# A planned attention-and-MLP block: another static order, zero products also ahead of side work, a norm chain without its copy, and a last tile whose norm and last product come in pieces

## The chip, the cores and the metric

The kernel runs on one core of one Trainium2 chip. The metric is the time of the whole execution on the device in microseconds, as the median of its runs. The engines are called as in the profile: PE is TensorE (matrix products, with PEld for its weight loads), ACT is ScalarE (activation functions), DVE is VectorE, POOL is GpSimd, and SP is SyncE, whose queue (SPq) issues nearly all transfers.

## The reference

One layer of a transformer with a grouped key and value (one for 32 heads) and a gated MLP; everything is bfloat16, with 2048 tokens of width 640.

```python
def _A_ref(x, wq, wk, wv, wo):          # H = 32 heads of Dh = 20, one k and one v for all
    q = (x @ wq).reshape(B, S, H, Dh).transpose(0, 2, 1, 3)
    k = x @ wk
    v = x @ wv
    scores = einsum("bhqd,bkd->bhqk", q, k) * (Dh ** -0.5)
    p = softmax(scores, axis=-1)
    o = einsum("bhqk,bkd->bhqd", p, v)
    return o.transpose(0, 2, 1, 3).reshape(B, S, H * Dh) @ wo
def _B_ref(x, w_gate, w_up, w_down):    # Dm = 640, Df = 1536
    return einsum("bsf,fd->bsd", gelu(x @ w_gate) * (x @ w_up), w_down)
x = A_x
h = x + _A_ref(layernorm(x), ...)
out = h + _B_ref(layernorm(h), ...)
```

## The kernel before

**Tiles and passes.** The tokens are cut into 16 tiles of 128 (`t`). A tile has two passes (`h` = 0, 1) of 16 heads, so there are 32 passes. In a pass the scores of the tile's queries against 16 blocks of 128 keys (`kt`) are formed in units: a unit is four heads against one block of keys, a matrix product on 32 rows of PE that fills one PSUM bank of 512 columns (line 940). Four units, one in each group of 32 rows, make a quad.

**Two ways of taking the exponential.** Most quads go to ACT: an activation Exp over two or three banks at once (line 1046, into `pbuf`). The string `D_QUADS` gives for each pass how many of the 16 quads go to DVE instead. There one TENSOR_SCALAR per unit (line 996) writes the bits of a power of two as integers (`dbuf`), and two shifted copies of the whole quad are made (`D_SHIFT`; line 1007 on DVE, or line 1011 on POOL for as many copies of a pass as `SHARE` allows), so that a weighted sum of three powers approximates the exponential. The products with the values (line 1160) then take one product per ACT quad and three per DVE quad; each is four matmuls on 32 columns of PE that run beside each other, added up in one PSUM bank.

**The rest of a tile** is called side work: the projection to q (two tiles ahead), the output projection and residual (lines 1265 to 1271), the second layer norm, the gate, up and down products (line 583 records all of these, since a helper `strips` issues them), the GELU by a tanh on ACT (line 1325) with its polynomial and its products on POOL or DVE (lines 1283 and 1285; `Z_POOL` and `H_POOL` choose by tile). Three operands per tile are transposed by a DMA from SP's queue: `onT<-oN` ahead of the output projection, `xnT<-xn_tmp` after the norm, `hhT<-g_us` ahead of the down product.

**The order.** Nothing is dynamic. A planner in the kernel's file (`_Sched.schedule`) takes every task with an estimated duration, simulates the five engines, and writes one fixed order for each. Its choices are steered by strings with one digit per pass: `PATIENCE`, `MARGIN`, `MARGIN_2` and `URGENT` (how long PE waits for score products, and what goes first), `D_AHEAD` and `D_BEFORE_END` (where a pass's DVE units are put among the cycles of score products), and by `LAG`, one digit per tile (0.05 us each, added to what the side work of that tile waits for in the plan). On the chip each engine runs its order, and a task waits on semaphores for what it needs. A PE task that is put too early therefore holds up everything behind it.

**Zero products.** Where the planner sees PE little used, it puts in a product of zeros (`filler`, four matmuls, planned at 0.215 us) that adds nothing to the open sum of the value products. The measure is `active`: PE's work in the last `WINDOW` = 3.42 us, where a score product counts as a quarter of its length. If it is below `least = 1.2 + 0.05 * FILL[phase]`, a zero product goes in, but only ahead of a score product (`t.cfg == "row"`).

**Norm.** The layer norm of a tile (`layer_norm`) is a chain over DVE and POOL: two BN_STATS and an aggregate on DVE, then on POOL a copy of the variance (`vb`, line 686, into `lnvb`), the addition of epsilon (`ve`, line 688), a power of one half (`pw`, line 690), and on DVE the reciprocal (`rc`) and the normalisation (`nm`, line 703).

**The last tile** (`last_tile`) has its own code: the output projection goes into the PSUM of the scores, the norm's chain is on DVE with the power on POOL (lines 1390 to 1402), PE transposes the result in two groups of 3 and 2 blocks (line 1420) that ACT and DVE evict (line 1427), and gate, up and down products run in three groups of four blocks of Df (lines 1445, 1472, 1477, 1454), the down product adding up in two halves of 320 columns, each of which is copied out and stored (lines 1488, 1490). Meanwhile PE works off what is left of tile 14's down product.

Of the kernel before, what the change touches and what calls it, by code (L numbers as in the profile page):

```python
# [6 lines left out]
ALU = mybir.AluOpType  # L7
# [4 lines left out]
P = 128  # L12
# [61 lines left out]
class _Sched:  # L74
# [8 lines left out]
    PATIENCE = "05456305540054532442603243443444"  # L83
    WINDOW, GAP = 3.42, 0.25
# [6 lines left out]
    FILL = "97755754644575535585755365355555"  # L91
# [45 lines left out]
    def schedule(self):  # L137
# [126 lines left out]
        while left:  # L264
# [202 lines left out]
def bass_sequential_preLN__grouped_kv_mqa__glu_gated_geglu__prompt_kernel(  # L467
# [74 lines left out]
    lnvb = sb("lnvb", [P, 4])  # L542
# [68 lines left out]
    LAG = "3434134353324532"  # L611
# [62 lines left out]
    def layer_norm(tag, t, src_deps, xnT_free, by_pe=None, fused=False):  # L674
# [11 lines left out]
        vb = add("pool", lambda e: e.tensor_copy(lnvb[:, ln.index:ln.index + 1], mv[:, ln.index, 1:2]), 0.2, [ag],  # L686
                 name=f"{tag}vb_{t}")
        ve = add("pool", lambda e: e.tensor_scalar(lnve[:, ln.index:ln.index + 1], lnvb[:, ln.index:ln.index + 1],
                                                   EPS, None, ALU.add), 0.2, [vb], name=f"{tag}ve_{t}")
        pw = add("pool", lambda e: e.tensor_tensor(lnden[:, ln.index:ln.index + 1],  # L690
                                                   lnve[:, ln.index:ln.index + 1], halfc[:], ALU.pow),
                 0.58, [ve, t_half], name=f"{tag}pw_{t}")
# [477 lines left out]
    URGENT = "45535357546755554446532554357655"  # L1170
# [106 lines left out]
    H_POOL = "1111111010011000"  # L1277
    Z_POOL = "0111010010011010"
# [72 lines left out]
    def last_tile(t, ont):  # L1351
# [45 lines left out]
        vb = add("dve", lambda e: e.tensor_copy(one(lnvb), mv[:, ln.index, 1:2]), 0.15, [ag], name=f"bvb_{t}")  # L1397
        ve = add("dve", lambda e: e.tensor_scalar(one(lnve), one(lnvb), EPS, None, ALU.add), 0.15, [vb], name=f"bve_{t}")
# [3 lines left out]
        nm = add("dve", lambda e: e.tensor_scalar(xn_tmp[:, xs.index, :], xh[:, t, :], mean(), one(lnr), ALU.subtract,  # L1402
# [37 lines left out]
        def job(wsb, i, bk):  # L1440
            def fn(e):
# [5 lines left out]
                return ins  # L1447
            return fn

        def down(i, j, c0, c1):  # L1450
            def fn(e):
                ins = None
                for fc in range(4 * i, 4 * i + 4):
# [272 lines left out]
```

## Time and profile before

| | us |
|---|---|
| median of 3 runs | 758.59 |
| lowest and highest run | 758.22 and 759.76 |
| the profiled execution's own time | 757.13 |
| span of its trace | 755.8 |
| PE busy | 719.4 (95%) |
| ACT busy | 724.4 (96%) |
| DVE busy | 667.9 (88%) |
| POOL busy | 271.7 (36%) |

The busy times come from one profiled execution; the span is from its first to its last instruction, and the execution's own time is 1.33 us longer. A busy PE is not PE at its peak, since the ends of matmuls are modelled, and four matmuls on 32 columns each can run beside each other. In the views, a time in brackets with an arrow is idle time of the engine just before the instruction, and names what ended it.

### The profile page before, as it was taken

What the parts mean: (1) busy time and instruction counts of PE and PEld (TensorE: products, weight loads), DVE (VectorE), ACT (ScalarE), POOL (GpSimd) and SP (SyncE); (2) the same over time, 40 slices, a digit from 0 to 9 for tenths busy, and PEclk for the clock granted to TensorE, in tenths of its full rate; (3) what the DMA queues carried; (4) which work ended last, traced back from release to release, by engine and by line L of the source; (5) the groups of instructions that cost most, each with busy time, mean ns of one, the idle gap of its engine ahead of it and who ended that gap; (6) DMA issues with size and microseconds to landing.
All of it is one profiled execution on the core that took longest, in us unless ns stands there. A gap on an engine that the chain in (4) does not pass through costs nothing.

```text
span 755.8 us, 24045 instructions
## 1 busy us (share of the span) xinstructions
PE 719.4 (95%) x10730; PEld 260.0 (34%) x10730; DVE 667.9 (88%) x1245; ACT 724.4 (96%) x698; POOL 271.7 (36%) x291
## 2 busy tenths in 40 slices
PE   9898999999998999999999999999999989999987
PEld 4422233333332333333333323333342323323336
DVE  8789999999998889999998899999989899888963
ACT  6999999999999999999999999999999999999982
POOL 5431315225355254324563234423232532450220
PEclk9999999999999999999999999999999999999999
DMA  7667002010113012111201102201130111010110
GB/s 181 128 218 192 10 10 45 11 30 6 31 33 45 19 23 43 27 30 10 45 3 40 33 11 46 41 20 24 23 55 20 16 20 23 19 31 19 35 33 20
DMA packets 79952, 31.53 MB, mean 42 GB/s; under 512 B 70880, under 2 KB 78560, under 8 KB 79840
## 3 DMA queue, kind: packets, MB, share of 16 engines
q1 hardware_dynamic: 78528, 29.86, 18.6%
q8 instruction: 85, 1.39, 0.7%
q10 hardware_dynamic: 1312, 0.05, 0.1%
q14 instruction: 27, 0.22, 0.1%
HBM read 10.21 MB, written 2.62 MB: 17 GB/s over the span
## 4 chain that ended last, share of the span: by engine, by line
ACT 44%; PE 41%; DVE 9%; DMA 3%; POOL 1%; issue 1%; SPq 0%; DVEq 0%
ACT pbuf L1046 42%; PE ps L583 15%; PE ps L940 14%; PE ps L1160 11%; DVE dbuf L996 3%; DVE dbuf L1007 2%; DMA onT<-oN 2%; ACT g_z L1325 1%; PE ps L1445 1%; DMA xh<-in_A_x_dram 1%; DMA xnT<-xn_tmp 1%; DVE stats L680 1%; DVE xn_tmp L703 1%; DVE stats L682 1%; POOL g_us L1285 0%
## 5 line engine op out<-in xcount | busy, mean ns | idle before, releaser
L1046 ACT ACTIVATE pbuf<-ps 128x1024 bf16<-128x1024 f32 (+1 forms) x656 | 696.6, 1218 | 9.6 <-PE ps L940 8.2
L996 DVE TENSOR_SCALAR dbuf<-ps 128x512 int16<-128x512 f32 x532 | 350.2, 680 | 40.5 <-PE ps L940 36.7
L940 PE MATMUL ps<-qT,kT 32*128 32x512 bf16 x2048 | 281.7, 387 | 16.9 <-ACT pbuf L1046 11.2
L940 PEld LDWEIGHTS ps<-qT,kT 32*128 32x128 bf16 x2048 | 73.6, 91 | 255.6 <-ACT pbuf L1046 189.7
L1007 DVE TENSOR_SCALAR dbuf<-dbuf 128x2048 int16<-128x2048 int16 x216 | 147.6, 700 | 0.8
L1160 PE MATMUL ps<-pbuf,v_ext 128*32 128x512 bf16 (+3 forms) x2052 | 144.5, 331 | 2.7 <-ACT pbuf L1046 1.7
L1160 PE MATMUL ps<-dbuf,v_w 128*32 128x512 bf16 x1596 | 139.6, 383 | 4.6 <-DVE dbuf L1007 3.3
L1011 POOL TENSOR_TENSOR dbuf<-dbuf,shifts 128x1024 int32<-128x1024 int32 x50 | 97.3, 1954 | 100.6 <-DVE dbuf L996 100.6
L1313 POOL TENSOR_TENSOR g_z<-g_gs 128x512 bf16<-128x512 bf16 x45 | 49.5, 1101 | 122.4 <-DVE g_gs L1311 122.1
L583 PE MATMUL ps<-wg_sb,xnT 128*32 128x512 bf16 x900 | 71.1, 389 | 0.5 <-DVE dbuf L996 0.2
L1160 PEld LDWEIGHTS ps<-pbuf,v_ext 128*32 128x32 bf16 x2052 | 44.9, 95 | 70.7 <-issue 49.2
L583 PE MATMUL ps<-wd_sb,hhT 128*32 128x320 bf16 x1440 | 67.6, 301 | 0.1
L583 PE MATMUL ps<-wu_sb,xnT 128*32 128x512 bf16 x900 | 66.8, 382 | 0.5 <-DVE dbuf L996 0.4
L1160 PEld LDWEIGHTS ps<-dbuf,v_w 128*32 128x32 bf16 x1596 | 39.5, 95 | 42.8 <-DVE dbuf L1007 15.7
L1285 POOL TENSOR_TENSOR g_us<-g_z,g_us 128x512 bf16<-128x512 bf16 x30 | 34.6, 1178 | 38.3 <-DVE g_z L1328 33.3
L1186 POOL TENSOR_TENSOR oN<-oT,rL 128x320 bf16<-128x320 f32 x30 | 21.8, 728 | 63.1 <-DVE rL L1181 63.0
L686 POOL CAST lnvb<-mv 128x1 bf16<-128x1 f32 x31 | 9.7, 313 | 96.0 <-DVE mv L684 95.9
L583 PEld LDWEIGHTS ps<-wd_sb,hhT 128*32 128x32 bf16 x1440 | 31.9, 96 | 25.3 <-issue 15.3
L1319 DVE SCALAR_TENSOR_TENSOR g_us<-ps,g_gs 128x512 bf16<-128x512 f32 x45 | 30.6, 679 | 6.0 <-PE ps L583 5.9
L1285 POOL TENSOR_TENSOR g_z<-g_z,g_gs 128x512 bf16<-128x512 bf16 x24 | 27.5, 1172 | 19.7 <-DVE g_z L1322 19.7
L583 PE MATMUL ps<-wo_sb,onT 128*32 128x320 bf16 x600 | 30.3, 304 | 4.5 <-DMA onT<-oN 3.8
L1311 DVE CAST g_gs<-ps 128x512 bf16<-128x512 f32 x45 | 30.5, 678 | 3.0 <-PE ps L583 2.7
(99 smaller groups left out, 407.9 us busy)
## 6 DMA issues: line engine op xcount, KB each, us to landing
out_dram<-xh SPq DMA_DIRECT2D x15, 160.0 KB, 2.1
wg_sb<-in_B_w_gate_dram SPq DMA_DIRECT2D x1, 1920.0 KB, 10.6
wu_sb<-in_B_w_up_dram SPq DMA_DIRECT2D x1, 1920.0 KB, 15.0
wd_sb<-in_B_w_down_dram SPq DMA_DIRECT2D x1, 1920.0 KB, 19.7
xh<-in_A_x_dram SPq DMA_DIRECT2D x2, 640.0 KB, 6.7
xh<-in_A_x_dram SPq DMA_DIRECT2D x3, 320.0 KB, 3.3
wq_sb<-in_A_wq_dram SPq DMA_DIRECT2D x2, 400.0 KB, 4.4
wo_sb<-in_A_wo_dram SPq DMA_DIRECT2D x1, 800.0 KB, 5.8
```

The costliest lines, as they stand in the source:

```text
L583: ins = e.matmul(out[r, :], lhs[:, r], rhs, start=start, stop=stop, tile_position=(0, 32 * b))
L940: return e.matmul(bk.rearrange("p (g n) -> p g n", g=4), kT4[r, kt * P:(kt + 1) * P], qT[r, main_q[t].index, 4 * h:4 * h + 4, :], start=Tr ...
L996: quad["bits"].append(sc.add("dve", lambda e: e.tensor_scalar(part(seg, w=slice(512 * item[0], 512 * item[0] + 512)), bk(), D_BIAS, 0.0, A ...
L1007: dep = [sc.add("dve", lambda e, j=j, s=s: e.tensor_scalar(part(s), part(seg), D_SHIFT[j], None, ALU.add), 0.602, bits + t_shift, prio=0.4 ...
L1011: dep[0].other = (lambda e, j=j, s=s: e.tensor_tensor(pairs(s), pairs(seg), shifts[:, j - 1:j].to_broadcast([P, 1024]), ALU.add), 2.03)
L1046: exps.append(sc.add("act", lambda e, w0=w0, w1=w1, to=to: e.activation(pbuf[:, to:to + w1 - w0], ps[:, w0:w1], ACT.Exp, scale=EXP_SCALE), ...
L1160: ins = e.matmul(ps[32 * b:32 * b + 32, PVB * 512 + a:PVB * 512 + a + n].rearrange("p (a n) -> p a n", n=32), x[2], span.rearrange("p (a n ...
L1186: onorm[(t, h)] = c = sc.add(by, lambda e: e.tensor_tensor(oN[:, otk.index, h * (D // 2):(h + 1) * (D // 2)].rearrange("p (g l d) -> p l g ...
L1285: return [sc.add("pool", lambda e, c=slice(512 * j, 512 * j + 512): e.tensor_tensor(out[:, k.index, c], a[:, k.index, c], b[:, k.index, c] ...
L1311: ge = sc.add("dve", lambda e, col=col, bk=bk: e.tensor_copy(g_gs[:, gsl.index, col], bk()), d_ps(512), [gm], prio=EVAC + pr, rel=[ax], na ...
L1313: sqt = sc.add("pool", lambda e, col=col: e.tensor_tensor(g_z[:, gsl.index, col], g_gs[:, gsl.index, col], g_gs[:, gsl.index, col], ALU.mult),
L1319: uts.append(sc.add("dve", lambda e, col=col, bk=bk: e.scalar_tensor_tensor(g_us[:, gsl.index, col], bk(), 0.5, g_gs[:, gsl.index, col], A ...
```

## The change

1. The strings of the order are replaced by others: `PATIENCE`, `FILL`, `LAG`, `SHARE`, `D_QUADS`, `D_AHEAD`, `D_BEFORE_END`, `MARGIN`, `MARGIN_2`, `URGENT`, `H_POOL`, `Z_POOL`. Summed over their digits, `D_QUADS` goes from 133 to 132 quads on DVE (two passes one fewer, one pass one more), `SHARE` from 72 to 73, `FILL` from 170 to 208, `H_POOL` from 10 to 9 tiles on POOL and `Z_POOL` from 8 to 6.
2. A zero product may also go ahead of side work and of value products, where PE is planned to be idle for at least `THIN` = 0.34 us and `active` is below `least`.
3. The copy of the variance (`vb`, line 686 on POOL, and `bvb`, line 1397 on DVE in the last tile) is left out; the addition of epsilon reads the aggregate itself.
4. In the last tile the normalisation (line 1402) is two instructions, over blocks 0 to 2 and 3 to 4, and each group of transposes waits for its own.
5. In the last tile the last of the three groups of `hh` (line 1477) is two instructions of two blocks, and the last down product goes in two rounds of two blocks for both halves of the columns, in place of four blocks for one half and then the other.

```diff
-    PATIENCE = "05456305540054532442603243443444"
-    WINDOW, GAP = 3.42, 0.25
+    PATIENCE = "00351403540064331442615343334144"
+    WINDOW, GAP, THIN = 3.42, 0.25, 0.34
-    FILL = "97755754644575535585755365355555"
+    FILL = "99875555686475667664669886669866"
...
-                if t.__class__ is not int and t.cfg == "row" and active(at - self.WINDOW, at) < least and (
-                        at - free[e] >= self.GAP or active(at - self.WINDOW, at) < least - .08):
+                row = t.__class__ is not int and t.cfg == "row"
+                if active(at - self.WINDOW, at) < least and (
+                        row and (at - free[e] >= self.GAP or active(at - self.WINDOW, at) < least - .08)
+                        or at - free[e] >= self.THIN):
...
-    LAG = "3434134353324532"
+    LAG = "3434134331414422"
...
-        vb = add("pool", lambda e: e.tensor_copy(lnvb[...], mv[:, ln.index, 1:2]), 0.2, [ag], ...)
-        ve = add("pool", lambda e: e.tensor_scalar(lnve[...], lnvb[...], EPS, None, ALU.add), 0.2, [vb], ...)
+        ve = add("pool", lambda e: e.tensor_scalar(lnve[...], mv[:, ln.index, 1:2], EPS, None, ALU.add), 0.22, [ag], ...)
...
-    SHARE = "12222423023232117222224236222200"
-    D_QUADS = "05554545454445445445445345453533"
-    D_AHEAD = "32422242222234232546422253223222"
-    D_BEFORE_END = "33333354431333254533334514334233"
-    MARGIN = "21323542445401555611434734356014"
-    MARGIN_2 = "56668364266545553771246624333655"
+    SHARE = "12232313014532217222238231112200"
+    D_QUADS = "05554445454445445445435445453533"
+    D_AHEAD = "22330242222434232546022333425232"
+    D_BEFORE_END = "45433355442243254533214314134243"
+    MARGIN = "21611452443404555516244634153004"
+    MARGIN_2 = "46868244276567553777325124313355"
...
-    URGENT = "45535357546755554446532554357655"
+    URGENT = "45635337646555554445463474357555"
...
-    H_POOL = "1111111010011000"
-    Z_POOL = "0111010010011010"
+    H_POOL = "1110101001001110"
+    Z_POOL = "0011100000011010"
...
-        vb = add("dve", lambda e: e.tensor_copy(one(lnvb), mv[:, ln.index, 1:2]), 0.15, [ag], name=f"bvb_{t}")
-        ve = add("dve", lambda e: e.tensor_scalar(one(lnve), one(lnvb), EPS, None, ALU.add), 0.15, [vb], ...)
+        ve = add("dve", lambda e: e.tensor_scalar(one(lnve), mv[:, ln.index, 1:2], EPS, None, ALU.add), 0.16, [ag], ...)
...
-        nm = add("dve", lambda e: e.tensor_scalar(xn_tmp[:, xs.index, :], xh[:, t, :], mean(), one(lnr), ...), 0.45, ...)
+        nms = [add("dve", lambda e, c=slice(128 * c0, 128 * c1): e.tensor_scalar(
+            xn_tmp[:, xs.index, c], xh[:, t, c], mean(), one(lnr), ALU.subtract, ALU.mult), 0.08 + 0.06 * (c1 - c0),
+            ...) for c0, c1 in ((0, 3), (3, ND))]
...
-            tp_t = add("pe", tp, 0.07 * (c1 - c0), [nm, t_ident], acq=[ps_s], rel=[xs], name=f"btp_{t}")
+            tp_t = add("pe", tp, 0.07 * (c1 - c0), [nms[c0 > 0], t_ident], acq=[ps_s], rel=[xs], name=f"btp_{t}")
...
-        def downs(i):
-            for j, c0, c1 in halves_:
-                dn[j] = add("pe", down(i, j, c0, c1), 0.56, [hhs[i], dma_wd, again] + ([dn[j]] if i else []), ...)
+        def downs(i, k=4):
+            for f in range(0, 4, k):
+                for j, c0, c1 in halves_:
+                    dn[j] = add("pe", down(4 * i + f, 4 * i + f + k, j, c0, c1), 0.14 * k, ...)
...
-        downs(2)
+        downs(2, 2)
```

More of the change, by code (lines that the diff above doesn't have):

```diff
@@ L1448, in job, with down @@
             return fn
-        def down(i, j, c0, c1):
+        def down(f0, f1, j, c0, c1):
             def fn(e):
                 ins = None
-                for fc in range(4 * i, 4 * i + 4):
+                for fc in range(f0, f1):
                     ins = e.matmul(acc(j), hhT[:, hh.index, fc, :], wd_sb[:, fc, c0:c1], start=False,
```

34 lines of the change are left out of this document (18 added, 16 removed).

## The prediction

> **What bounds the kernel now.** I read the page's busy shares and the shares of the chain that ended last first, then the groups of instructions by line.
>
> ```profile
> PE 719.4 (95%) x10730; PEld 260.0 (34%) x10730; DVE 667.9 (88%) x1245; ACT 724.4 (96%) x698; POOL 271.7 (36%) x291
> ACT 44%; PE 41%; DVE 9%; DMA 3%; POOL 1%; issue 1%; SPq 0%; DVEq 0%
> L1046 ACT ACTIVATE pbuf<-ps 128x1024 bf16<-128x1024 f32 (+1 forms) x656 | 696.6, 1218 | 9.6 <-PE ps L940 8.2
> L996 DVE TENSOR_SCALAR dbuf<-ps 128x512 int16<-128x512 f32 x532 | 350.2, 680 | 40.5 <-PE ps L940 36.7
> L1007 DVE TENSOR_SCALAR dbuf<-dbuf 128x2048 int16<-128x2048 int16 x216 | 147.6, 700 | 0.8
> L1283 DVE TENSOR_TENSOR g_z<-g_z,g_gs 128x1536 bf16<-128x1536 bf16 x7 | 6.6, 946 | 0.0
> L583 PE MATMUL ps<-halves,zeros 128*32 128x512 bf16 x188 | 16.6, 444 | 1.1 <-DVE halves L665 1.1
> ```
>
> ACT and PE share the chain, but they are not alike: the exponentials keep ACT busy for 696.6 us, and ACT waited only 9.6 us ahead of them. So the time is ACT's work, plus the few places where ACT ran dry, plus a head and a tail in which ACT is not the bound. DVE waited 40.5 us ahead of its exponentials, so it is not the bound. The timeline of ACT gives the places where it ran dry:
>
> ```profile
> 23.15 48.63 ACT L1046 ACTIVATE pbuf<-ps 128x1024 bf16<-128x1024 f32 x45 [0.99 <-PE ps L940]
> 244.01 1.99 ACT L1046 ACTIVATE pbuf<-ps 128x1024 bf16<-128x1024 f32 x2 [1.87 <-PE ps L940]
> 246.76 2.38 ACT L1046 ACTIVATE pbuf<-ps 128x1536 bf16<-128x1536 f32 x2 [0.77 <-PE ps L940]
> 249.53 10.17 ACT L1046 ACTIVATE pbuf<-ps 128x1024 bf16<-128x1024 f32 x9 [0.40 <-PE ps L940]
> 558.96 50.32 ACT L1046 ACTIVATE pbuf<-ps 128x1024 bf16<-128x1024 f32 x48 [0.63 <-PE ps L940]
> 618.50 41.75 ACT L1046 ACTIVATE pbuf<-ps 128x1536 bf16<-128x1536 f32 x39 [0.90 <-PE ps L940]
> 667.30 26.44 ACT L1046 ACTIVATE pbuf<-ps 128x1024 bf16<-128x1024 f32 x25 [0.50 <-PE ps L940]
> 694.40 13.24 ACT L1046 ACTIVATE pbuf<-ps 128x1024 bf16<-128x1024 f32 x12 [0.66 <-PE ps L940]
> ```
>
> In the brackets is the idle time just before. After the head seven waits make 5.73 us (1.87 + 0.77 + 0.40 + 0.63 + 0.90 + 0.50 + 0.66). To see why, I asked for the busy time of each engine in stretches of 3.41 us; the columns are the length, busy time of PE, PEld, DVE, ACT and POOL with counts, the granted TensorE clock, DMA share and GB/s:
>
> ```profile
> 241.15:244.56 3.41, 1.45 (x26) 0.55 (x22) 1.14 (x3) 1.54 (x3) 3.25 (x2) 1.00 0.47 87
> 244.56:247.97 3.41, 3.41 (x32) 0.80 (x30) 2.36 (x5) 2.64 (x3) 0.00 (x0) 0.50 0.00 0
> 613.20:616.61 3.41, 2.14 (x25) 0.60 (x21) 3.41 (x7) 3.33 (x4) 0.00 (x0) 1.00 0.25 48
> 616.61:620.02 3.41, 3.15 (x31) 0.78 (x35) 2.89 (x6) 2.52 (x4) 0.00 (x0) 0.50 0.03 7
> 660.99:664.40 3.41, 1.88 (x31) 0.53 (x23) 2.39 (x5) 3.41 (x4) 2.11 (x2) 1.00 0.25 48
> 664.40:667.81 3.41, 3.41 (x30) 0.49 (x22) 1.87 (x4) 2.83 (x4) 3.41 (x4) 0.50 0.02 5
> 729.25:732.66 3.41, 2.51 (x34) 0.62 (x26) 1.65 (x2) 3.41 (x4) 0.00 (x0) 1.00 0.17 55
> 731.20:734.61 3.41, 1.73 (x21) 0.45 (x21) 0.07 (x1) 3.33 (x4) 0.00 (x0) 1.00 0.62 118
> ```
>
> Three times the clock falls to 0.50 for 3.41 us, each time behind a stretch in which PE was busy for 1.45, 2.14 or 1.88 us. These stretches begin at 244.56, 616.61 and 664.40, which are 372.05 and 47.79 us apart, or 109.0 and 14.0 times 3.413: the stretches lie on a fixed grid. That explains the last two rows. The stretch from 731.20 is as empty (1.73) as those that cost the clock, but it does not lie on this grid; the grid's stretch there, from 729.25, held 2.51, and the clock stayed. In an execution whose grid lies otherwise this place may cost the clock, and others may not.
>
> [...]
>
> **The three drops have different causes.** These are rows of the timeline:
>
> ```profile
> 236.93 1.44 SPq L1331 DMA_TRANSPOSE hhT<-g_us  x1
> 238.42 1.60 SPq L1193 DMA_TRANSPOSE onT<-oN  x1
> 243.32 0.32 PE L583 MATMUL ps<-wo_sb,onT 128*32 128x320 bf16 x4 [1.96 <-DMA onT<-oN]
> 614.47 0.40 PE L1160 MATMUL ps<-dbuf,v_w 128*32 128x512 bf16 x4 [0.83 <-DVE dbuf L1007]
> 616.87 0.62 PE L1160 MATMUL ps<-dbuf,v_w 128*32 128x512 bf16 x4 [0.69 <-DVE dbuf L1007]
> 662.59 0.39 PE L940 MATMUL ps<-qT,kT 32*128 32x512 bf16 x3 [0.91 <-ACT pbuf L1046]
> 733.66 0.40 PE L1160 MATMUL ps<-pbuf,v_ext 128*32 128x512 bf16 x4 [0.95 <-ACT pbuf L1046]
> ```
>
> The first is a wait of PE that was not planned: SP's queue issued the transpose for `onT` right behind the one for `hhT`, so it was late, and the score products stood behind the output projection. The second comes from gaps ahead of value products, where the planner so far puts no zero product; the gap at 733.66 is of this kind too. The third has gaps ahead of score products, where zero products went in, but too few.
>
> **The change, part by part.** *One quad more on ACT.* The digits of `D_QUADS` sum to 132 in place of 133, so ACT takes 512 − 132 = 380 quads in place of 379: 1520 units in place of 1516. At 696.6 / 1516 = 0.460 us a unit, four units cost **+1.84 us**, wholly on the path, since ACT has no slack. DVE saves four exponentials (350.2 / 532 = 0.658) and two shifted copies (147.6 / 216 = 0.683), 4.0 us, and gets back three products that leave POOL (one of `H_POOL`, two of `Z_POOL`; 3 x 0.946 = 2.8 us); I put both at nothing, because DVE's 40.5 us of waiting take them. If DVE were late, PE would wait for its copies as at 614.47, 0.83 us each time.
>
> *The clock.* A higher `FILL` (170 to 208, a mean of 0.06 us more demanded per window) and zero products ahead of value products speak to the second and the third drop, not to the first. ACT lost 0.90 and 0.50 behind those two, and 0.77 + 0.40 behind the first one beyond the wait itself: 2.57 us. I take all of it as gone and put back half a drop of the first kind (0.6): **−1.97 us**, between 0 (the places move, the number stays) and −2.57.
>
> *The empty place at 731.* The profiled execution did not pay for it (its time is 757.13 against a median of 758.59). Of grids laid at random most would meet it. At half clock 3.41 us of PE cost between 0 and 1.71; the other drops cost ACT 0.50 to 1.17. I take **−0.7 us** against the median; here the zero products go ahead of value products.
>
> ```profile
> PE ps L583 <- DMA onT<-oN: 3.8, 3, 2.0
> ```
>
> *Late transposes.* ACT's waits of 1.87, 0.63 and 0.66 at 244, 559 and 694, 3.16 in all, come right behind places where PE met the output projection's transpose late; the list of waits (total, times, longest) has three such. The order is drawn anew and nothing in the change prices the queue otherwise, so I expect three again, but near the two common sizes: 3 x 0.65 = 2.0, **−1.16 us**. Bounds: none left (−3.16), or three like the first (+2.45, and their drops).
>
> *The copy of the variance* goes out of the chain; in the head, rows of the chain of waits:
>
> ```profile
> 4.54 0.20 POOL lnvb L686
> 4.74 0.08 issue
> 739.22 0.16 DVE L1397 CAST lnvb<-mv 128x1 bf16<-128x1 f32 x1
> 741.25 0.34 PE L1420 MATMUL ps<-ident,xn_tmp 128*128 128x128 bf16 x3
> 741.92 0.28 PE L1420 MATMUL ps<-ident,xn_tmp 128*128 128x128 bf16 x2 [0.33 <-DVE xh L1344]
> 740.43 0.45 DVE L1402 TENSOR_SCALAR xn_tmp<-xh,mv,lnr 128x640 bf16<-128x640 bf16 x1
> 750.38 2.34 PE L1454 MATMUL ps<-wd_sb,hhT 128*128 128x320 bf16 x16
> 750.59 0.69 DVE L1477 TENSOR_TENSOR hhT<-ps,g_gs 128x512 bf16<-128x512 f32 x1 [2.63 <-PE ps L1445]
> 752.22 0.98 ACT L1488 ACTIVATE xh<-ps 128x320 bf16<-128x320 f32 x2 [2.15 <-PE ps L1454]
> ```
>
> Tile 0's norm ends the wait for the first score product, so 0.20 + 0.08 = **−0.28 us**. Later tiles lie beside ACT's work: nothing, or at most another part of the 0.99 that ACT waits at 23.15.
>
> *The last tile.* The norm's chain loses 0.16 (739.22) and the first transposes could start 0.45 x 2/5 = 0.18 earlier. But the normalisation ended at 740.88 and the first transposes started at 741.25: PE was still in tile 14's down product. The second transposes waited for its residual (line 1344). So this gains nothing unless the down product is further on by then: 0 to −0.34. The last product in pieces gains nothing either: PE's 16 down matmuls run without a break from 750.38, and `hh`, over at 751.28, is covered by the eight of the group before (half of 2.34: to 751.55). It even costs a little: the first half of the columns is complete two matmuls (2.34 / 16 x 2 = 0.29) later, and its copy-out (0.98 / 2 = 0.49) stands ahead of the second: 0 to +0.2. Together **−0.1 us**.
>
> *The zero products' own cost.* The 188 matmuls are 47 zero products, at 16.6 / 47 = 0.35 us of PE. Perhaps 25 more go in, each into a planned gap of 0.25 us or more; where the work comes earlier than planned, it waits. Between 0 and 25 x 0.35 = 8.8; ACT's reserve of filled banks covers most: **+0.2 us**.
>
> Sum: 1.84 − 1.97 − 0.7 − 1.16 − 0.28 − 0.1 + 0.2 = −2.17 us. All terms but the third belong to the profiled execution (757.13 to about 755.7); with the third, against the median of 758.59, that is **756.4 us**.
>
> **The rivals.** *The gaps are not what drops the clock.* [...] As a mechanism of this kernel: the longest wait in the rows above is 1.96, drops would fall where they like, and terms two and three vanish: 758.59 + 1.84 − 1.16 − 0.28 − 0.1 + 0.2 = 759.1. Against it: each drop stands right behind one of the emptiest stretches. 0.10, counted as no change (within 0.2%, 1.5 us, about what a measurement of this kernel can tell).
>
> *The gains just pay for the quad.* The waits at late transposes stay at 3.16 and one whole drop remains: 756.4 + 1.16 + 0.6 = 758.2. For it: ACT's floor rises for certain, the rest is hoped for. 0.12, no change.
>
> *Late transposes take over (slower).* Each wait like the one at 243.32 costs 1.87 plus the drop behind it, 1.17: 3.04. No zero product helps, as the plan does not see the wait. With two, the term is 6.08 − 3.16 = +2.92 and the residual drop of 0.6 is in it: 759.9; with three, 762.9. It decides from the third. For it: three waits were there before, and `LAG` falls (52 to 46 over its digits). Against: only one of them was large. 0.17.
>
> *Zero products in the way (slower).* If 25 cost a third of their 0.35 each, +2.9 in place of +0.2, with the transposes as before (+1.16): 760.3. For it: PE is at 95% and has 41% of the chain. Against: their place is where PE idles. 0.07.
>
> **How the numbers follow.** Forecast 0.54, at 753.2 to 757.1 by itself; no change 0.10 + 0.12 = 0.22; slower 0.17 + 0.07 = 0.24. The low end has no late transpose and no drop left: 1.84 − 3.16 − 2.57 − 0.9 (at 731) − 0.5 (head) − 0.1 = −5.4, 753.2. The high end lies between two and three late transposes, at 760.6, with about one chance in ten above.
>
> **What would show it.** ACT's exponentials at some 698.4 us; the clock at 1.00 nearly throughout; zero products ahead of value products, more than 47 in all; the row `lnvb` gone and the first exponential 0.28 earlier; the last product no earlier relative to its last up product. Wrong would be: ACT's idle time ahead of its exponentials above the present 9.6 us, a clock at 0.50 behind a wait for `onT`, or zero products right ahead of score products for which ACT waits.

## The result: slower by 1.0%, and the profile after

The changed kernel takes 766.74 us as the median of six runs (764.06 to 768.46); the kernel before, on the same chip, 759.17 (756.01 to 760.5). The ratio is 1.0100, with a 95% interval of 1.0072 to 1.0128. The prediction was 756.4, with a range that ended at 760.6. Two executions of later runs, far longer than all others of their kernel (1012.05 and 2017.19 us), are left out of every number below.

The profiled execution of the changed kernel took 767.15 us, its span 765.7. From its page: the busy shares, the shares of the chain that ended last, and groups of instructions (busy time, mean ns of one, idle time just before them).

```profile
PE 723.7 (95%) x10754; PEld 263.7 (34%) x10754; DVE 675.0 (88%) x1242; ACT 727.6 (95%) x700; POOL 262.4 (34%) x252
ACT 44%; PE 30%; DVE 20%; DMA 3%; POOL 2%; issue 1%; SPq 0%; ACTq 0%
L1045 ACT ACTIVATE pbuf<-ps 128x1024 bf16<-128x1024 f32 (+1 forms) x658 | 700.0, 1221 | 17.3 <-PE ps L939 16.3
L1006 DVE TENSOR_SCALAR dbuf<-dbuf 128x2048 int16<-128x2048 int16 x213 | 156.5, 753 | 0.6
L1010 POOL TENSOR_TENSOR dbuf<-dbuf,shifts 128x1024 int32<-128x1024 int32 x51 | 102.0, 2005 | 97.9 <-DVE dbuf L995 97.9
L1312 POOL TENSOR_TENSOR g_z<-g_gs 128x512 bf16<-128x512 bf16 x45 | 53.9, 1197 | 129.3 <-DVE g_gs L1310 129.3
L584 PE MATMUL ps<-halves,zeros 128*32 128x512 bf16 x236 | 21.3, 426 | 1.1 <-DVE halves L666 1.1
```

Two rows of before that the prediction does not show are POOL's shifted copies and POOL's squares (a square is a step of the GELU's polynomial):

```profile
L1011 POOL TENSOR_TENSOR dbuf<-dbuf,shifts 128x1024 int32<-128x1024 int32 x50 | 97.3, 1954 | 100.6 <-DVE dbuf L996 100.6
L1313 POOL TENSOR_TENSOR g_z<-g_gs 128x512 bf16<-128x512 bf16 x45 | 49.5, 1101 | 122.4 <-DVE g_gs L1311 122.1
```

The span grew by 9.9 us. ACT's exponentials account for all of it: 3.4 us more of their own work (700.0 against 696.6) and 7.7 more of waiting ahead of them (17.3 against 9.6, which the prediction had named as a sign of being wrong). And more of the chain now runs through DVE: its share went from 9% to 20%. And here stands a line that should not have moved at all. DVE's shifted copies are the same instruction on the same shape, but the mean went from 700 to 753 ns, and POOL's copies and squares went from 1954 to 2005 and from 1101 to 1197. Something holds these instructions up while they run. Two places where that happens, from the timeline of the changed kernel:

```profile
303.55 4.65 ACT L1045 ACTIVATE pbuf<-ps 128x1536 bf16<-128x1536 f32 x4
304.97 0.44 DVE L702 TENSOR_SCALAR xn_tmp<-xh,mv,lnr 128x640 bf16<-128x640 bf16 x1
305.14 4.32 POOL L1010 TENSOR_TENSOR dbuf<-dbuf,shifts 128x1024 int32<-128x1024 int32 x2 [2.12 <-DVE dbuf L995]
305.33 2.38 DVE L1006 TENSOR_SCALAR dbuf<-dbuf 128x2048 int16<-128x2048 int16 x1
307.76 0.40 PE L1159 MATMUL ps<-pbuf,v_ext 128*32 128x512 bf16 x4 [1.38 <-DVE dbuf L1006]
309.43 1.45 ACT L1045 ACTIVATE pbuf<-ps 128x1536 bf16<-128x1536 f32 x1 [1.23 <-PE ps L939]
...
122.39 0.44 DVE L702 TENSOR_SCALAR xn_tmp<-xh,mv,lnr 128x640 bf16<-128x640 bf16 x1
122.56 1.17 POOL L1312 TENSOR_TENSOR g_z<-g_gs 128x512 bf16<-128x512 bf16 x1 [0.86 <-DVE g_gs L1310]
122.74 1.53 DVE L1006 TENSOR_SCALAR dbuf<-dbuf 128x2048 int16<-128x2048 int16 x1
```

At 305.14 POOL starts two copies, 0.19 us ahead of a DVE copy. The DVE copy lasts 2.38 us in place of 0.68. PE stands for 1.38 us ahead of the group of value products that needs it, the next score products are queued behind that group, and ACT runs dry for 1.23 us. The second place is the same with one of POOL's squares (1.53 us).

The lengths can be worked out, best at the second place. Undisturbed, a POOL square takes 1.04 us (the mean of 1041 ns in the first experiment below) and a DVE copy 0.68 (681 ns, the mean of the 207 copies of before that are not stretched). The square did not come first: DVE's normalisation (line 702) ran from 122.39 to 122.83, and the square, started in between, ended at 123.73, 0.90 after the end of the normalisation. The DVE copy ended at 124.27, 0.55 after the end of the square. So here each takes its own time, less about 0.14 us, from the moment that the other is done. The first place has the same chain: normalisation, POOL's first copy, DVE's copy. And it is so every time: each of the 27 stretched DVE copies of the two traces (9 before, 18 after) ends 0.55 us after the POOL instruction that it started beside, to within 0.01 us, whether the copy had by then run beside it for 0.18 us (from 677.60 in the trace of after) or for 1.83 (from 305.33). At half speed beside POOL, a copy that started 1.83 us ahead of POOL's end would have been over by then; in these 27 cases it had 0.55 of its 0.68 us left.

Before, 9 of DVE's 216 shifted copies are stretched, together by 4.2 us, six of them to more than 1 us; after, 18 of 213 are, by 14.4 us, 14 of them to more than 1 us.

Here a stall cost twice. These are stretches of 3.41 us of the changed kernel (length, then busy time of PE, PEld, DVE, ACT and POOL with counts, granted TensorE clock, DMA share, GB/s), and the timeline inside them:

```profile
582.04:585.45 3.41, 1.97 (x26) 0.43 (x22) 3.41 (x4) 2.57 (x3) 2.22 (x1) 1.00 0.02 5
585.46:588.87 3.41, 3.33 (x25) 0.65 (x21) 3.41 (x7) 2.02 (x2) 0.73 (x1) 0.53 0.01 2
588.87:592.28 3.41, 3.41 (x35) 0.84 (x36) 1.69 (x4) 2.65 (x3) 0.00 (x0) 0.50 0.01 2
```

```profile
584.86 0.40 PE L1159 MATMUL ps<-dbuf,v_w 128*32 128x512 bf16 x4 [1.36 <-DVE dbuf L1006]
585.55 1.54 PE L939 MATMUL ps<-qT,kT 32*128 32x512 bf16 x6
```

PE waits 1.36 us for a stretched copy, so its stretch holds 1.97 us of work, and the clock falls to 0.50 behind it, at 585.68, for 6.83 us, two stretches; six score matmuls then take 1.54 us. The trace of after_port below has no drop at this place.

### The profile page after: what moved, and what is told of

Its sections match the earlier page's. It is cut to its first block, busy times and chain, and to the rows that moved or that the text cites. A ratio compares the mean times of both kernels' runs of the same rounds, so it can differ in the third digit from the quotient of the medians.

```text
span 765.7 us, 24048 instructions
## 1 busy us (share of the span) xinstructions
PE 723.7 (95%) x10754; PEld 263.7 (34%) x10754; DVE 675.0 (88%) x1242; ACT 727.6 (95%) x700; POOL 262.4 (34%) x252
## 4 chain that ended last, share of the span: by engine, by line
ACT 44%; PE 30%; DVE 20%; DMA 3%; POOL 2%; issue 1%; SPq 0%; ACTq 0%
ACT pbuf L1045 43%; PE ps L939 10%; PE ps L584 10%; PE ps L1159 9%; DVE dbuf L995 7%; DVE dbuf L1006 5%; DMA hhT<-g_us 1%; ACT g_z L1324 1%; PE ps L1446 1%; DVE stats L681 1%; DVE stats L683 1%; DVE g_us L1318 1%; DVE xn_tmp L702 1%; DVE g_gs L1310 1%; DMA xh<-in_A_x_dram 1%
## 5 line engine op out<-in xcount | busy, mean ns | idle before, releaser
L1045 ACT ACTIVATE pbuf<-ps 128x1024 bf16<-128x1024 f32 (+1 forms) x658 | 700.0, 1221 | 17.3 <-PE ps L939 16.3
L995 DVE TENSOR_SCALAR dbuf<-ps 128x512 int16<-128x512 f32 x528 | 346.1, 682 | 46.7 <-PE ps L939 43.9
L939 PE MATMUL ps<-qT,kT 32*128 32x512 bf16 x2048 | 284.6, 387 | 19.6 <-ACT pbuf L1045 11.6
L1006 DVE TENSOR_SCALAR dbuf<-dbuf 128x2048 int16<-128x2048 int16 x213 | 156.5, 753 | 0.6
L1010 POOL TENSOR_TENSOR dbuf<-dbuf,shifts 128x1024 int32<-128x1024 int32 x51 | 102.0, 2005 | 97.9 <-DVE dbuf L995 97.9
L1312 POOL TENSOR_TENSOR g_z<-g_gs 128x512 bf16<-128x512 bf16 x45 | 53.9, 1197 | 129.3 <-DVE g_gs L1310 129.3
L584 PE MATMUL ps<-wg_sb,xnT 128*32 128x512 bf16 x900 | 68.5, 383 | 1.6 <-DVE dbuf L995 1.0
L687 POOL TENSOR_SCALAR lnve<-mv 128x1 bf16<-128x1 f32 x31 | 10.1, 324 | 90.7 <-DVE mv L685 90.5
L1284 POOL TENSOR_TENSOR g_us<-g_z,g_us 128x512 bf16<-128x512 bf16 x27 | 32.2, 1210 | 25.5 <-DVE g_z L1327 25.5
L584 PE MATMUL ps<-wq_sb,xnT 128*32 128x320 bf16 (+1 forms) x660 | 32.7, 298 | 0.3 <-DVE dbuf L995 0.3
```

What stands on the lines that cost most here:

```text
L584: ins = e.matmul(out[r, :], lhs[:, r], rhs, start=start, stop=stop, tile_position=(0, 32 * b))
L939: return e.matmul(bk.rearrange("p (g n) -> p g n", g=4), kT4[r, kt * P:(kt + 1) * P], qT[r, main_q[t].index, 4 * h:4 * h + 4, :], start=Tr ...
L995: quad["bits"].append(sc.add("dve", lambda e: e.tensor_scalar(part(seg, w=slice(512 * item[0], 512 * item[0] + 512)), bk(), D_BIAS, 0.0, A ...
L1006: dep = [sc.add("dve", lambda e, j=j, s=s: e.tensor_scalar(part(s), part(seg), D_SHIFT[j], None, ALU.add), 0.602, bits + t_shift, prio=0.4 ...
L1010: dep[0].other = (lambda e, j=j, s=s: e.tensor_tensor(pairs(s), pairs(seg), shifts[:, j - 1:j].to_broadcast([P, 1024]), ALU.add), 2.03)
L1045: exps.append(sc.add("act", lambda e, w0=w0, w1=w1, to=to: e.activation(pbuf[:, to:to + w1 - w0], ps[:, w0:w1], ACT.Exp, scale=EXP_SCALE), ...
```

## Experiments

**Theory.** The new order puts POOL's instructions right behind DVE's. The planner does keep them apart: it marks both with `port`, and `_Sched.schedule` has a lock that lets no POOL instruction of this kind overlap a DVE one. But it is only in the plan. On the chip POOL waits for its own inputs alone, and where they are there early, it starts ahead of the DVE copy that it was planned behind. `port` is the planner's word; the traces show that the one stands while the other runs (the 27 copies above), not why. In the plans, POOL starts directly (within 0.06 us) behind a DVE instruction of this kind 17 times before and 30 times after. **Rivals:** the zero products stand in the way; the clock falls in other places; the order is simply worse.

Since runs of one kernel differ by several microseconds with the granted clock, I also give the time at full clock. The lost time of a run is (1 − clock) x span; over all runs, within one kernel, each lost microsecond goes with 0.62 us of time. "At full clock" is the mean time less 0.62 times the mean lost time. It is an extrapolation: the slopes of single kernels with more than two runs lie between 0.35 and 1.02, and for kernels that lose over 10 us a slope of 0.35 or 0.8 would move it by 2 to 4 us. The kernels were run in four sets, those of the experiments on three chips, each with the kernel before beside it, so a ratio compares within a set, and a difference of two medians often does not. The kernel before, at full clock, is at 754.2, 753.9 and 753.6 in the three sets of the experiments.

| kernel | median us | ratio to before, 95% | mean lost us | at full clock |
|---|---|---|---|---|
| before | 757.4 to 759.2, by set | | 7.3 | 753.9 |
| after | 766.74 | 1.0100 (1.0072 to 1.0128) | 3.7 | 764.1 |
| after_port | 757.54 | 0.9975 (0.9950 to 1.0001) | 2.9 | 756.2 |
| before_port | 756.48 | 0.9981 (0.9955 to 1.0007) | 5.9 | 753.1 |
| after_no_zero | 767.20 | 1.0131 (1.0072 to 1.0191) | 10.2 | 760.2 |
| before_no_zero | 758.73 | 1.0004 (0.9981 to 1.0026) | 13.2 | 750.5 |
| after_port_copies | 764.09 | 1.0070 (1.0043 to 1.0098) | 3.8 | 761.3 |
| after_port_others | 762.37 | 1.0066 (1.0034 to 1.0098) | 5.7 | 759.7 |
| after_port_no_zero | 755.47 | 0.9987 (0.9953 to 1.0020) | 11.4 | 749.6 |
| before_port_tail | 755.27 | 0.9961 (0.9927 to 0.9996) | 4.3 | 752.7 |
| strings_only | 769.50 | 1.0149 (1.0088 to 1.0209) | 1.5 | 768.5 |
| old_strings | 769.66 | 1.0151 (1.0089 to 1.0213) | 3.5 | 767.5 |
| before_port_tail_vb | 755.13 | 0.9973 (0.9940 to 1.0006) | 5.0 | 752.6 |
| after_port_end_zero | 757.78 | 0.9987 (0.9958 to 1.0016) | 11.8 | 750.3 |

**after_port: the planned order of these instructions, kept by a wait.** Each POOL instruction of the lock's kind also waits for the DVE instruction that it was planned behind. The strings and the planned order are those of the changed kernel.

```diff
+        last_port = {"dve": None}
...
             if t.port:
+                if e == "dve":
+                    last_port[e] = t
+                elif last_port["dve"] is not None:
+                    t.extra.append(last_port["dve"])
                 lock[e] = at + t.dur + self.PORT
```

> [...] Theory A (collisions: POOL starts ahead of a DVE copy that the plan puts first, and DVE is held up): the long DVE copies (above 1 us) nearly go, and 5 to 8 us of the 7.6 us lost come back, 759 to 762 us. Theory B (the zero products delay real work): no change, 766 to 768. Theory C (the new order is worse in itself, by PE waits that have nothing to do with the port): no change, 766 to 768.

Groups of its page:

```profile
L1050 ACT ACTIVATE pbuf<-ps 128x1024 bf16<-128x1024 f32 (+1 forms) x658 | 697.8, 1227 | 13.0 <-PE ps L944 12.3
L1011 DVE TENSOR_SCALAR dbuf<-dbuf 128x2048 int16<-128x2048 int16 x213 | 144.1, 694 | 0.6
L1015 POOL TENSOR_TENSOR dbuf<-dbuf,shifts 128x1024 int32<-128x1024 int32 x51 | 96.2, 1893 | 102.8 <-DVE dbuf L1011 50.8
L1317 POOL TENSOR_TENSOR g_z<-g_gs 128x512 bf16<-128x512 bf16 x45 | 46.9, 1041 | 143.8 <-DVE dbuf L1011 65.8
```

And the place shown above, in its timeline:

```profile
306.81 0.69 DVE L1011 TENSOR_SCALAR dbuf<-dbuf 128x2048 int16<-128x2048 int16 x1
307.58 3.74 POOL L1015 TENSOR_TENSOR dbuf<-dbuf,shifts 128x1024 int32<-128x1024 int32 x2 [3.08 <-DVE dbuf L1011]
```

POOL now waits for the DVE copy (its groups name that line, L1011, as what ended their idle time), and this wait costs nothing that shows: DVE's copies fall from 156.5 to 144.1 us, POOL's from 102.0 to 96.2, its squares from 53.9 to 46.9. Of the 18 stretched copies six are left, 2.2 us too long in all, three of them longer than 1 us. The time falls by 9.2 us in the medians, from 766.74 to 757.54 (9.5 by the ratios), with a wait more for these POOL instructions and nothing less in the program. ACT's waiting falls only from 17.3 to 13.0 us, in a profiled execution that took 761.56, the longest of its runs. What the change lost against the kernel before is in these overlaps.

**before_port: the same wait in the kernel before.**

> The same added wait in the kernel before. Theory A: it has fewer collisions (10 stretched instructions, 4.3 us of DVE in all, against 19 and 15.2), so it gains 1 to 2 us, 757 to 758. Theories B and C: no change, 758.5 to 760.

The interval of the ratio, 0.9955 to 1.0007, holds no change; the median is 1 to 2 us lower. But the mechanism was not the expected one: eight of the nine stretched copies are still there, 3.6 us too long in all in place of 4.2. In the plans they have the other order: POOL's instruction comes first, and on the chip the DVE copy arrives before it is over. The added wait does not touch these; it mends only POOL instructions that start ahead of a DVE instruction planned before them, and of those the kernel before has one stretched copy and the changed kernel eleven. The six that are left in after_port are of the other order too. So this run shows that the wait by itself does not make a kernel faster by 9 us: it gives back what an order loses.

**after_port_copies and after_port_others: which of POOL's instructions.** The wait for POOL's shifted copies alone (names that begin with `ds`), and for all others alone.

```diff
-                elif last_port["dve"] is not None:
+                elif last_port["dve"] is not None and t.name.startswith("ds"):          # copies
+                elif last_port["dve"] is not None and not t.name.startswith("ds"):      # others
```

> The changed kernel with its order, and the added wait for the shifted copies on POOL alone (51 instructions). Three DVE copies were held up for 1.7 us each by these, 5.1 us in all. If each 1 us of DVE held up costs about 0.8 us (8 to 9 us for some 12 us with the full wait), some 4 us come back: 762 to 763.5. If the copies are all there is, 757 to 758; if they do nothing, 766 to 767.

> The complement: the added wait for the squares and products on POOL, not for its copies. Eight DVE instructions were held up for 0.75 to 0.96 us by these, 6.8 us in all. At the same price 5 us come back: 761 to 763; the two halves should add up to about the 9 us of the full wait. If the copies are all there is, 766 to 767.

Groups of the page with the wait for copies alone, and then for the others alone:

```profile
L1011 DVE TENSOR_SCALAR dbuf<-dbuf 128x2048 int16<-128x2048 int16 x213 | 151.4, 728 | 0.6
L1015 POOL TENSOR_TENSOR dbuf<-dbuf,shifts 128x1024 int32<-128x1024 int32 x51 | 96.2, 1892 | 106.6 <-DVE dbuf L1000 53.1
L1317 POOL TENSOR_TENSOR g_z<-g_gs 128x512 bf16<-128x512 bf16 x45 | 53.9, 1197 | 128.3 <-DVE g_gs L1315 128.3
```

```profile
L1011 DVE TENSOR_SCALAR dbuf<-dbuf 128x2048 int16<-128x2048 int16 x213 | 149.5, 719 | 0.6
L1015 POOL TENSOR_TENSOR dbuf<-dbuf,shifts 128x1024 int32<-128x1024 int32 x51 | 102.0, 2005 | 94.3 <-DVE dbuf L1000 94.3
L1317 POOL TENSOR_TENSOR g_z<-g_gs 128x512 bf16<-128x512 bf16 x45 | 46.7, 1039 | 143.5 <-DVE dbuf L1011 66.4
```

Each half mends its own rows (1892 and 1039) and leaves the other's (1197 and 2005). At full clock both count: of the 7.9 us the copies give back 2.8 and the others 4.4, 7.2 together. By the ratios it is 2.3 and 2.6 of 9.5, and each interval still overlaps that of the changed kernel, so how the gain is shared is not settled. The wait for copies alone missed its expectation (764.09 against 762 to 763.5).

**after_no_zero and before_no_zero: without zero products.** The zero products inside the value sums (37 after, 24 before) are not issued; the planned order is otherwise unchanged. This keeps the 22 or 23 in the first 15 us.

```diff
+            if t.name == "filler":
+                continue
```

> The changed kernel with the same order, but the zero products inside the value sums (37 of them) are not issued; the 22 of the start and the end stay. Theory B: 4 to 7 us come back, 760 to 763. Theory A: nothing comes back; the clock falls in more places, 767 to 770. Theory C: as A.

> The kernel before without its 24 zero products inside the value sums. Theory B: faster by 2 to 4 us, 755 to 757. Theories A and C: as before or slower by up to 2 us from more drops of the clock, 759 to 761.

No gain in either: 1.0131 against 1.0100 for the changed kernel, 1.0004 for the kernel before. The zero products do two things that nearly cancel. Without them the mean granted clock falls from 0.995 to 0.987 after and from 0.990 to 0.983 before; and at full clock the kernels would be 3.9 and 3.4 us faster. So here a zero product is worth its place for the clock. Its cost, some 0.10 to 0.14 us of time each (3.9 / 37 and 3.4 / 24), is only an estimate: at 0.35, the slope of before_no_zero's own runs, the 3.4 us vanish. In the trace of after_no_zero 18 copies are stretched by 14.4 us as with the zero products, so these do not trigger the collisions. The rival that the zero products took the 10 us falls.

**after_port_no_zero and after_port_end_zero: the same with the wait.** The second issues only the zero products planned from 715 us on.

```diff
-            if t.name == "filler":
+            if t.name == "filler" and t.start < 715:
                 continue
```

> The changed kernel with its order and the full added wait, without the 37 zero products inside the value sums. Without the wait, leaving them out made the run shorter by some 4 us at full clock and lost some 6.5 us more to half clock, so the median did not move. If the price of the zero products comes from PE alone, the same holds here: 757 to 759, with a mean clock near 0.987. If it came through collisions that they trigger, they are free here, and the time without them is 759 to 762.

> The changed kernel with its order and the added wait, keeping only the zero products that the plan has after 715 us, at the end of the value sums. Without any inside the value sums it took 755.5, with all of them 757.5. If the drop behind the end's empty place costs 1 to 2 us and the zero products there cost nothing, 753.5 to 754.5; if these cost as much as the others (about 0.13 us each at full clock), 755 to 756.

All three versions with the wait lie within their intervals of each other (0.9975, 0.9987, 0.9987 of before). Both expectations missed: 755.47 is below what either reading allowed, and 757.78 above. Zero products are a draw here: without them 8.5 to 9 us more of clock are lost, and at full clock, by the extrapolation, the time is some 6 us shorter.

**strings_only and old_strings: parts of the change alone.** The kernel before with all the new strings and nothing else; and the changed kernel with all the old strings.

```diff
-    PATIENCE = "05456305540054532442603243443444"      # strings_only; old_strings is the reverse
+    PATIENCE = "00351403540064331442615343334144"
... (and the eleven other strings)
```

> The kernel before with the new strings alone (no zero products ahead of side work, the copy of the variance and the last tile as before). The planner then draws another order, which by its own times ends 12 us later than the order of before and 10 us later than the changed kernel's. If the strings carry the change, as a setting that is good or bad in itself, the time is near the changed kernel's: 764 to 768. If a string only fits the code it was chosen with, the time follows the plan: about 770 to 778, later by 10 us or more than the kernel before.

> The changed kernel with the strings of before. By its own times this plan ends 13 us later than the order of before. If the rest of the change (zero products ahead of side work, no copy of the variance, the last tile in pieces) is harmless in itself, one would expect 757 to 760; if a string only fits the code it was chosen with, 770 to 778.

Both have medians above that of the whole change, 769.5 and 769.66, from two runs each, and their intervals overlap its own. Their plans already end at 758.1 and 759.7, against 746.2 for the kernel before and 748.2 for the changed one, and their spans are 10.2 and 9.6 us longer than the plan. That is as much as before (755.8 − 746.2 = 9.6), while the changed kernel is 17.5 longer. So their time is in the plan. That the strings are fitted to one exact code would explain it; neither half can be judged alone, and the split by parts failed. It leaves a measure: span less plan shows what the planner doesn't know. But the trace of strings_only has 13 stretched copies, by 10.5 us in all, at a span no further above its plan than before, where they make 4.2. So the sum of the stretching is no price; what a stretched copy costs depends on where it falls.

**before_port_tail: the empty place ahead of the last tile.** In before_port, three and one zero products go ahead of the last two value products.

```diff
+    last_pv = [t for t in sc.order["pe"] if t.name.startswith("pv_")][-2:]
+    for t, n in zip(last_pv, (3, 1)):
+        for k in range(n):
+            f = sc.add("pe", ..., 0.0, sc.filler[2], name="tail_filler", cfg="col")
+            ...
+            sc.order["pe"].insert(sc.order["pe"].index(t), f)
```

> The kernel before with the added wait, and four zero products more, three ahead of the last but one and one ahead of the last product of the value sums (where PE waits 0.95 and 0.52 us for ACT). If the drop of the clock behind that empty place costs some 2 us (a tail of 23.4 us where it happens against 21.3 where not) in three runs out of four, 754.5 to 755.5; if the place costs nothing, 756.5 as without them.

Stretches, first of before_port, then of this kernel, with the columns as above:

```profile
726.37:729.78 3.41, 2.27 (x26) 0.54 (x26) 1.65 (x2) 3.41 (x4) 0.00 (x0) 1.00 0.18 42
729.38:732.79 3.41, 2.16 (x14) 0.71 (x13) 0.71 (x1) 1.98 (x2) 0.00 (x0) 0.56 0.60 115
```

```profile
729.38:732.79 3.41, 2.68 (x33) 0.66 (x33) 0.18 (x1) 3.41 (x4) 0.00 (x0) 1.00 0.62 118
```

From the end of the last exponential to the end of the span it took 23.4 us in before_port, with the clock at half, and 21.1 here. The kernel before, whose clock was at 1.00 there, has 21.3. So the drop, here of two stretches, costs some 2 us where it falls. That the four zero products are what kept the clock is not shown: in before_port it fell at 729.78, before PE's wait of 0.95 us had ended, behind the stretch from 726.37, and the grid of stretches lies otherwise in the two traces. The ratio is the lowest of all, 0.9961 (0.9927 to 0.9996), but the interval overlaps that of before_port.

**before_port_tail_vb: the copy of the variance left out as well.** The addition of epsilon reads the aggregate, and `vb` and `bvb` go out of the fixed order.

> The kernel before with the added wait and the four zero products at the end of the value sums, and without the copy of the variance (POOL's 31 and DVE's one), every other instruction in its place. In the head tile 0's norm is 0.28 us shorter, in the last tile 0.16 on DVE: if both are on the path, 754.8 to 755.0 against 755.3; if other work is late there anyway, 755.3. The first exponential at 10.1 in place of 10.4 would show the head's part.

```profile
9.96 1.45 ACT L1051 ACTIVATE pbuf<-ps 128x1536 bf16<-128x1536 f32 x1 [0.39 <-PE ps L945]
```

The first exponential starts 0.34 us earlier than in before_port_tail (10.30), about as the prediction's −0.28 had it. The median is 755.13 against 755.27, in another set (by the ratios 0.9973 against 0.9961), which at this spread says nothing about 0.3 us.

## Why the prediction was wrong, step by step

**The failed step** is in the part on the quad: "I put both at nothing, because DVE's 40.5 us of waiting take them", of what moves between DVE and POOL. It counted how much work moved and not when it falls; the sum has no term for where the new order puts DVE's and POOL's work against each other. POOL has nearly the same number of copies and squares (51 and 45, against 50 and 45); what is new is that eleven of DVE's copies, where it was one, are held up by a POOL instruction that the plan puts behind them. DVE's mean reserve is no cover for a copy that lasts 2.38 us with a value product, the next score products and ACT behind it. The step even had the price, 0.83 each "if DVE were late", and no count for it. What it left out measures 764.1 − 756.2 = 7.9 us at full clock, more than every term of the sum. None of the four rivals had it. The page of before did show it: 700 ns as the mean of a copy that undisturbed takes about 0.68 us, and 1954 and 1101 for POOL's where 1893 and 1041 are undisturbed.

**The other terms.** *The quad* agrees in size but is not shown by itself: at full clock with the wait the changed kernel is 2.3 us behind the kernel before (756.2 − 753.9) and 3.1 behind before_port, which has the same wait (753.1); its plan ends 2.0 later; the term was +1.84. The prediction had ACT's exponentials at 698.4 us: they take 697.8 in after_port, and 700.0 in the changed kernel. DVE's copies fell by three, 216 to 213, not by two, since `SHARE` gives one more to POOL.

*The clock and the place at 731*, −1.97 and −0.7, were about right in sum: the mean lost clock went from 7.3 to 3.7 us, or 0.62 x 3.6 = 2.2 us of time, and in after_port to 2.9, 2.7 us. In the tail of before_port the drop lasted two stretches and cost about 2 us, where the prediction had 0 to 1.71 for one stretch and took 0.7. The stretches from 582.04 show one reason why the lost clock did not go to nothing: a collision made a drop of its own. The grid itself is in the traces: the three drops of before last 3.413 us each, and the two of after, which start at 568.61 and 585.68, 3.413 and 6.826; their starts are 5.0 times 3.413 apart, beside the 109.0 and 14.0 of before. The reading that went with the grid was incomplete. In the trace of before the grid's next stretch, from 732.65, held only 1.95 us of PE work, less than the 2.14 ahead of the drop at 616.61, and the clock stayed. So PE's busy time alone does not tell where the clock falls.

*Zero products* were mis-sized. I expected 25 more; 12 came (59 in all against 47; 13 more inside the value sums and one fewer at the start), and only 7 of the 37 in value sums stand directly ahead of value products or side work in the plan. I put their cost near nothing (+0.2); at the estimate of 0.10 to 0.14 us each, 12 would cost 1.2 to 1.7 us. The rival that put them in the way named a third of 0.35 us each, about the size of that estimate, but at that size they are a small part of what was lost.

*The rival "the gaps are not what drops the clock"* falls, since leaving zero products out lowers the clock in both kernels (0.995 to 0.987 and 0.990 to 0.983). The prediction counted for it that PE's longest wait in its rows is 1.96 us; no run shows how long a gap must be for the clock to fall, and here a drop stands behind a stretch with 1.97 us of PE work, whose longest gap was 1.36 (584.86).

*Late transposes.* One large wait for `onT` remains, and a large one for `hhT`, of another transpose, is new. From the timelines of the changed kernel and of its ACT, and the stretches of 3.41 us around the second:

```profile
66.74 1.29 SPq L1192 DMA_TRANSPOSE onT<-oN  x1
71.93 0.86 PE L584 MATMUL ps<-wo_sb,onT 128*32 128x320 bf16 x20 [1.79 <-DVE dbuf L995]
73.17 1.94 ACT L1045 ACTIVATE pbuf<-ps 128x1024 bf16<-128x1024 f32 x2 [1.54 <-PE ps L939]
562.09 1.55 SPq L1330 DMA_TRANSPOSE hhT<-g_us  x1
567.29 1.27 PE L584 MATMUL ps<-wd_sb,hhT 128*32 128x320 bf16 x32 [2.21 <-DVE mv L685]
569.06 1.02 ACT L1045 ACTIVATE pbuf<-ps 128x1024 bf16<-128x1024 f32 x1 [1.00 <-PE ps L939]
571.65 12.96 ACT L1045 ACTIVATE pbuf<-ps 128x1024 bf16<-128x1024 f32 x12 [1.57 <-PE ps L939]
```

```profile
565.19:568.60 3.41, 1.31 (x35) 0.86 (x35) 2.62 (x6) 2.87 (x3) 1.10 (x2) 1.00 0.22 15
568.61:572.02 3.41, 3.41 (x38) 1.17 (x39) 1.62 (x4) 1.39 (x2) 0.00 (x0) 0.50 0.00 0
```

The DVE instruction named ahead of the projection had long been done: the transpose for `onT` was issued at 66.74 and landed 5.1 us later, at 71.84. That for `hhT` was issued at 562.09 and landed at 567.25, 5.2 later; the product behind it started at 567.29 and reads nothing of the DVE instruction that is named. Behind the first ACT lost 1.54 us, and 0.41 behind a smaller one at 701.64: 1.95 in place of 3.16, where the prediction had 2.0. But behind the second PE waited 2.21 us, the clock fell, and ACT lost 1.00 + 1.57 = 2.57 us more. The trace of before has no such wait for `hhT`; that of after_port has it again (2.24 us), so it belongs to the new order and is no part of what the added wait gives back. So the gain of the term did not come, and the rival for the slow side, though not the main cause, was there in part, at a transpose that it did not name.

*The head* went the other way. Timelines of before and of after:

```profile
10.41 1.45 ACT L1046 ACTIVATE pbuf<-ps 128x1536 bf16<-128x1536 f32 x1 [0.39 <-PE ps L940]
```

```profile
9.53 0.28 PE L857 MATMUL ps<-ident,q_tok 128*128 128x128 bf16 x2 [0.46 <-DVE q_tok L842]
9.74 0.61 PE L584 MATMUL ps<-halves,zeros 128*32 128x512 bf16 x8
10.73 1.45 ACT L1045 ACTIVATE pbuf<-ps 128x1536 bf16<-128x1536 f32 x1 [1.12 <-PE ps L939]
```

The norm did end 0.3 us earlier, but in the new order DVE has more of the next tiles' norms ahead of its half of q (the cast started at 8.78 before and at 9.17 after), PE waits for it, and two zero products stand ahead of the first score product. The first exponential is 0.32 later, for a term of −0.28. That leaving out the copy is worth the 0.28 by itself is seen in before_port_tail_vb.

*The last tile* gained more than the −0.1. Timelines of before and after: the last exponentials, the eviction of the first transposes, and the issue of the last two stores.

```profile
729.90 4.62 ACT L1046 ACTIVATE pbuf<-ps 128x1536 bf16<-128x1536 f32 x4
741.63 0.49 ACT L1427 ACTIVATE xnT<-ps 128x384 bf16<-128x384 bf16 x1 [0.70 <-PE ps L1420]
752.68 1.86 SPq L1490 DMA_DIRECT2D out_dram<-xh  x2
```

```profile
736.40 8.72 ACT L1045 ACTIVATE pbuf<-ps 128x1536 bf16<-128x1536 f32 x8
751.77 0.49 ACT L1428 ACTIVATE xnT<-ps 128x384 bf16<-128x384 bf16 x1 [0.16 <-PE ps L1421]
763.08 1.37 SPq L1496 DMA_DIRECT2D out_dram<-xh  x2
```

From the end of the last exponential (734.52 and 745.12) to that eviction it is 7.11 us before and 6.65 after, so the norm without its copy and in two pieces gave 0.46, where I had put 0 to 0.34. Counted from there, the first store is issued 0.26 later than before (11.05 and 11.31 us), close to the two matmuls of 0.29 in the prediction; but the two issues are over sooner (1.37 us in place of 1.86), so that the last ends 0.23 earlier, where I had put 0 to +0.2 of loss. Together that is the 0.7 us by which the tail is shorter (21.3 and 20.6 us).

**The sum with the measured terms:** at full clock +2.3 with the wait (the quad, the later head, the shorter tail, the late transposes and the added zero products are all in it) and +7.9 from the overlaps, and −2.2 from the clock: +8.0, against 7.6 in the medians. These are differences of one table, so they add up by construction and check nothing. What stays open: how the 2.3 us divide, what a zero product costs, and what each string does.

## What to carry to other kernels

Where a planner keeps instructions of two engines apart, as here DVE's and POOL's, that order belongs into semaphores: in the changed kernel POOL started ahead of its plan at eleven DVE copies, and a wait gave back 9.2 us. A wait on one side holds one order only: here DVE copies that come too early for POOL were still held up, eight of nine in before_port. Before moving work between engines, look for lines whose mean is above their undisturbed duration (here 753 ns against 681), and find the overlap that stretches them; the 40.5 us that DVE waited ahead of its exponentials did not cover a copy of 2.38 us with a chain behind it. Work put in to hold the clock must be weighed against its own time: here it was a draw.

## What the runs showed of the hardware

A DVE copy of 0.68 us took 2.38 when a POOL copy had started 0.19 ahead of it, and 1.53 beside a POOL square. All 27 stretched copies of the two traces end 0.55 us after the end of the POOL instruction. It works the other way as well: the square that started while DVE normalised took 1.17 us in place of 1.04 and ended 0.90 after the normalisation.

The same kernel on different executions ran from 754.6 us at a mean granted clock of 0.995 to 764.4 at 0.982 (74 runs of the kernel before). The second lost 10 us more of clock, which at 0.62 is 6 of the 9.7 us between them.
